# Vector-times-matrix products of a decode step: weights as the moving operand in column groups, one block transpose a layer, and two output banks

## The chip, the cores and the metric

The kernel runs on one core of a Trainium2 chip. The metric is the device time of one execution in microseconds (us), taken as the median of several runs. A separate execution is recorded by the hardware profiler; its span runs from the first to the last instruction. Engines are named as in the profile: PE (TensorE matmuls), PEld (TensorE weight loads), DVE (VectorE), ACT (ScalarE), POOL (GpSimd) and SP (SyncE, which here issues nearly all DMA transfers).

## The reference, cut to what matters

Two batch rows (B = 2, one new token each) go through an attention block with a long cache (A) and an MLP mixer (B); a gate mixes both. D = 1024, 32 heads of 128, 16384 cached positions, F = 3584, all in bf16.

```python
def _A_ref(x, k_cache, v_cache, wq, wo):
    q = (x @ wq).reshape(B, 1, 32, 128).transpose(0, 2, 1, 3)
    scores = jnp.einsum("bhqd,bhkd->bhqk", q, k_cache) * (128 ** -0.5)
    o = jnp.einsum("bhqk,bhkd->bhqd", softmax(scores), v_cache)
    return o.transpose(0, 2, 1, 3).reshape(B, 1, 4096) @ wo

def _B_ref(x, w1, w2, w3, w4):
    h = gelu(layernorm(x) @ w1)
    # g0..g3: the four quarters of h, each shifted by one or two steps along a sequence of length 1
    x1 = x + concatenate([g0, g1, g2, g3]) @ w2
    return x1 + gelu(layernorm(x1) @ w3) @ w4

g = sigmoid((A_x * gate_w).sum(-1))
out = g * A(A_x) + (1 - g) * B(A_x)
```

With a sequence of length 1 every shifted quarter is zero, and the kernel uses a zero tile for that input (`shT`).

## The kernel before, in words

The caches are 537 MB of the 573 MB that are moved. Work is cut into 32 **units** u = (pair of heads, batch row), each with 8.39 MB of K and 8.39 MB of V. SBUF holds one large tile `mem` of five **cells** of 32 KB a partition. A K or V block fills two cells: K of even units cells 0 and 1, of odd units cells 1 and 2; V cells 3 and 4 (V of unit 30 cells 0 and 1). The weights borrow the cells early on: `wq` cells 3 and 4, `w1` and `w2` cell 2, then `w3` cells 3 and 4, then `w4` the same two.

Every load stands in one queue, SP's, in the order of the program; a load waits on SP until the cells that it fills have been read, and those behind it wait too. The order is: wq (L125), x and gate weights (L127, L129), w1, w2 (L226), K0 (L97), w3 in two halves (L226), K1, the first rows of wo (L428), w4 in two halves (L226), K2, V0 in two halves (L104), K3, V1 (L100), K4 and so on. At the end stand V30, V31 in nine pieces (`load_v_pieces`, L112: seven of 1 MB and two of 0.5 MB) and the last four tiles of wo (`load_wo_last`, L436).

The main loop runs over n = 0 to 31. For unit n `score_chunks` transposes K on DVE in 32 x 32 blocks (L462, eight chunks a unit) and multiplies it on PE (L468); `softmax_a` to `softmax_c` transpose the scores on DVE (L489), exchange maxima over a product with a matrix of ones (L499), take the exponentials on ACT (L507) and sum (L521 or L529). `pv(n - 2)` multiplies the probabilities with V (L543): eight probability columns are stationary, V moves 512 columns at a time, and four such products go to four groups of 32 output partitions of the bank `oacc`. `pv_rows` (L559, L565) picks the wanted parts out of that bank on DVE; a product with `hsel` (L585, L590) turns them into columns, `OT`; and `wo_project` (L441) adds `OT` times two rows of wo to the output sum `arow`, in four groups of 256 columns that share one PSUM bank.

The small layers are what the change is about. **q** (L268) is computed with blocks of wq as the stationary operand and the two columns of x moving: 256 products into a tile of columns, then four products with a selection matrix `sel` (L281) and two copies (L292) that lay q out for the score weights. **LinearT** (w1 to w4, L233) works the same way, one 128 x 128 block stationary at a time; `compute(k, c0, c1)` does some output columns c of one half k of the rows, and its calls for w3 and w4 lie between the softmax steps of units 0 and 1. `mlp_post4` (L402) adds the MLP's result into `arow` over a product with an identity.

In the last unit, `pv_last` does V31's first three pieces as moving operand (L543), and the other six as stationary operand, 128 x 128 at a time (L612), each into the same two columns; `OT` of the last pair (L619) then releases `wo_project` for the pairs 14 and 15. Each of the four wo tiles is waited for by its own group of four products. The sum leaves PSUM in two halves, one on DVE (L677) and one on ACT (L678), and goes out over two queues (L680).

The tile framework arranges each engine's instructions at build time; on PE they don't always follow the order of the program (some products of `lin3` stand between score products of unit 0).

Of the kernel before, what the change touches and what calls it, by code (L numbers as in the profile page):

```python
# [10 lines left out]
FP32 = mybir.dt.float32  # L11
# [12 lines left out]
def kernel(  # L24
# [74 lines left out]
    def load_v(u):  # L99
        nc.sync.dma_start(out=region(v_cell[u], NJ * Dh), in_=cache_rows(A_v_cache, u))  # L100

    def load_v_half(u, k):
        at = slice(k * CELL, (k + 1) * CELL)
        nc.sync.dma_start(out=region(v_cell[u], NJ * Dh)[:, at], in_=cache_rows(A_v_cache, u)[:, at])  # L104

    PIECES = [32] * 7 + [16] * 2
    assert sum(PIECES) == NJ

# [29 lines left out]
    ones_f = const.tile([P, P], FP32)  # L138
    nc.vector.memset(ones_f[:], 1.0)

    sel = const.tile([P, 4, Q4, QP], BF16)
    nc.gpsimd.memset(sel[:], 0.0)
    for v in range(4):
        w, e = divmod(v, 2)
        nc.gpsimd.affine_select(
            out=sel[:, v],
            in_=sel[:, v],
            compare_op=ALU.not_equal,
            fill=1.0,
            base=-(2 * QP * w + e),  # L150
            pattern=[[0, Q4], [-2, QP]],
            channel_multiplier=1,
        )
    mask4 = const.tile([P, Q4], BF16)
    nc.gpsimd.memset(mask4[:], 1.0)
    nc.gpsimd.affine_select(
# [46 lines left out]
    for k in range(NP):  # L203
        t = const.tile([P, NJ // 4, 2, 4], BF16, name=f"pt{k}")
        nc.gpsimd.memset(t[:], 0.0)
        pts.append(t)

    class LinearT:

        def __init__(self, W, actT, name, cell, offset, nparts=1):  # L210
            self.actT = actT
            K, self.N = W.shape
            self.R = K // P
            self.C = self.N // P
            self.rows = self.R // nparts
            self.src = W.rearrange("(p r) n -> p (r n)", p=P)

            self.at = [(cell + k) * CELL + offset for k in range(nparts)]
            self.acc = mlp.tile([P, self.C, B], FP32, name=f"{name}_acc")

        def part(self, k):
            return mem[:, self.at[k] : self.at[k] + self.rows * self.N]

        def load(self, k=0):
            n = self.rows * self.N
            nc.sync.dma_start(out=self.part(k), in_=self.src[:, k * n : (k + 1) * n])  # L226

        def compute(self, k, c0, c1):
            wc = self.part(k).rearrange("p (r n) -> p r n", n=self.N)
            ps = misc_psum([P, c1 - c0, B])  # L230
            for c in range(c0, c1):
                for r in range(self.rows):
                    nc.tensor.matmul(  # L233
                        ps[:, c - c0, :],
                        lhsT=wc[:, r, :].rearrange("p (m c) -> p c m", c=self.C)[:, c, :],
                        rhs=self.actT[:, k * self.rows + r, :],
                        start=(r == 0),
                        stop=(r == self.rows - 1),
                    )
            acc = self.acc[:, c0:c1, :]  # L240
            if k == 0:
                nc.vector.tensor_copy(out=acc, in_=ps[:])
            else:
                nc.vector.tensor_tensor(out=acc, in0=acc, in1=ps[:], op=ALU.add)

    xn1T = mlp.tile([P, KC, B], BF16)
    hT = mlp.tile([P, KC, B], BF16)
# [5 lines left out]

    lin1 = LinearT(B_w1, xn1T, "w1", 2, 0)
    lin2 = LinearT(B_w2, shT, "w2", 2, KC * D)
    lin3 = LinearT(B_w3, xn2T, "w3", 3, 0, 2)
    lin4 = LinearT(B_w4, h2T, "w4", 3, 0, 2)
    lin1.load()
    lin2.load()
    load_k(0)  # L260
# [1 line left out]
    xT = const.tile([P, KC, B], BF16)  # L262
    nc.vector.tensor_copy(out=xT[:], in_=xin[:].rearrange("p b r -> p r b"))  # L263

    qps = misc_psum([P, H, B])
    for h in range(H):
        for r in range(KC):
            nc.tensor.matmul(  # L268
                qps[:, h, :],
                lhsT=wq_t[:, r, h * Dh : (h + 1) * Dh],  # L270
                rhs=xT[:, r, :],
                start=(r == 0),
                stop=(r == KC - 1),
            )
    lin3.load(0)
    lin3.load(1)
    qT = const.tile([P, H, B], BF16)
    nc.vector.tensor_copy(out=qT[:], in_=qps[:])
    qdps = misc_psum([P, 4, H * B])
    for v in range(4):  # L280
        nc.tensor.matmul(  # L281
            qdps[:, v, :],
            lhsT=sel[:, v].rearrange("p a k -> p (a k)"),
            rhs=qT[:].rearrange("p h b -> p (h b)"),
            start=True,
            stop=True,
        )

    qd = const.tile([P, HP, B, 4], BF16)
    for e in range(2):  # L290
        rows = slice(e * HALF, (e + 1) * HALF)
        nc.vector.tensor_copy(  # L292
            out=qd[rows],
            in_=qdps[rows].rearrange("p v (hp e b) -> p hp e b v", e=2, b=B)[:, :, e],
        )
    qdu = qd[:].rearrange("p hp b v -> p (hp b) v")

    def write_qw(u):
# [82 lines left out]
        layernorm_T(x1T[:], xn2T[:], "ln2")  # L381


    NQ = D // Q4
    arow_t = rps.tile([P, NQ], FP32, name="arow")
    nc.vector.memset(arow_t[:], 0.0)
    arow = [arow_t[QP * k : QP * k + B, :] for k in range(Q4)]

    def mlp_post4():

        omg = mlp.tile([P, B], FP32, name="omg")
        nc.vector.tensor_scalar(
            out=omg[:], in0=g_rep[:], scalar1=-1.0, scalar2=1.0, op0=ALU.mult, op1=ALU.add
        )
        nc.vector.tensor_tensor(out=bT[:], in0=lin4.acc[:], in1=x1T[:], op=ALU.add)
        nc.vector.tensor_tensor(
            out=bT[:], in0=bT[:], in1=omg[:].unsqueeze(1).to_broadcast([P, KC, B]), op=ALU.mult
        )
        W = NQ // KC
        for k in range(Q4):  # L400
            for c in range(KC):
                nc.tensor.matmul(  # L402
                    arow[k].rearrange("b (m c) -> b c m", c=KC)[:, c, :],
                    lhsT=bT[:, c, :],
                    rhs=ident_f[:, k * W : (k + 1) * W],
                    start=(c == 0),
                    stop=False,
                    skip_group_check=True,
                )
# [27 lines left out]

    def wo_project(hp):
        for r in range(2):
            for k in range(Q4):  # L440
                nc.tensor.matmul(  # L441
                    arow[k],
                    lhsT=OT[:, hp, r, :],
                    rhs=wo_tiles[hp, r][:, k * NQ : (k + 1) * NQ],
                    start=False,
                    stop=(hp == HP - 1 and r == 1),
                    skip_group_check=True,
                )
# [154 lines left out]
    def pv_last(u):  # L603
        hp, b = units[u]
        ot = misc_psum([P, 2])
        moving = sum(PIECES[:3]) // 4
        pv_moving(u, 0, moving, moving)
        red = pv_rows(u, mask4m)
        nc.tensor.matmul(ot[:], lhsT=red[:, 0:Dh], rhs=hsel[:], start=True, stop=False)
        V = v_view(u)  # L610
        for j in range(4 * moving, NJ):
            nc.tensor.matmul(  # L612
                ot[:],
                lhsT=V[:, j, :],
                rhs=pts[u % NP][:, j // 4, :, j % 4],
                start=False,
                stop=(j == NJ - 1),
            )
        nc.vector.tensor_tensor(out=OT[:, hp, :, b], in0=ot[:], in1=rinvs[u % NP][:], op=ALU.mult)  # L619
        for k in range(HP - LASTP, HP):  # L620
            wo_project(k)

    compute_gate()
    layernorm_T(xT[:], xn1T[:], "ln1")
    lin1.compute(0, 0, lin1.C)
    mlp_post1()
    lin2.compute(0, 0, lin2.C)
    mlp_post2()

    for n in range(NU):  # L630
# [6 lines left out]
        softmax_a(n)  # L637
        if n == 0:
            load_wo_pair(0)
            lin3.compute(0, 0, FC // 2)  # L640
            softmax_b(n)
            lin3.compute(0, FC // 2, FC)
            lin4.load(0)
            softmax_c(n)
            lin3.compute(1, 0, FC)
            lin4.load(1)
            gelu_T(lin3.acc[:], h2T[:], FC)
        elif n == 1:
            lin4.compute(0, 0, KC // 2)
            softmax_b(n)  # L650
            lin4.compute(0, KC // 2, KC)
            load_v_half(0, 0)
            softmax_c(n)
            lin4.compute(1, 0, KC)
            load_v_half(0, 1)
            mlp_post4()
        else:
            pv(n - 2)
            if n < NU - 1:
                load_v(n - 1)  # L660
            else:
                load_v_pieces(NU - 1)
            pv_end(n - 2)
            if n == NU - 1:
                load_wo_last()
            softmax_b(n)
            softmax_c(n)
# [3 lines left out]
    pv_end(NU - 2)  # L671
    pv_last(NU - 1)

    out_row = mlp.tile([P, NQ], BF16)
    used = slice(0, QP * (Q4 - 1) + B)
    half = NQ // 2
    nc.vector.tensor_copy(out=out_row[used, 0:half], in_=arow_t[used, 0:half])  # L677
    nc.scalar.activation(out=out_row[used, half:NQ], in_=arow_t[used, half:NQ], func=ACTF.Copy)  # L678
    for b, queue in ((0, nc.sync), (1, nc.scalar)):
        queue.dma_start(  # L680
            out=out[b, 0].rearrange("(k n) -> k n", k=Q4),
            in_=out_row[b : b + QP * (Q4 - 1) + 1 : QP, :],
        )


# [28 lines left out]
```

## Time and profile before

| | before |
|---|---|
| time, median of 3 runs | 1341.07 us (1340.96 to 1341.09) |
| the profiled execution's own time | 1341.09 us |
| its span | 1339.4 us |
| mean granted TensorE clock | 0.785 |
| busy: PE, PEld, DVE, ACT, POOL | 768.8, 351.9, 705.1, 105.2, 15.2 us |
| moved by DMA | 573.33 MB, mean 428 GB/s |
| queue q1 (SP's transfers) | 99.3% of 16 engines' span |

The profile gives busy time by engine, the span in 40 slices of 33.5 us each, the DMA queues, the chain of waits that ended last, and groups of instructions by line. The timeline lists instructions in order of time, neighbours merged: start, duration, engine, line, operation, output <- input, shape, count, and in brackets the idle time before with what ended it. `SPq` and `ACTq` are transfers issued by those engines; the duration there is that of issuing. A table by windows gives busy time, granted clock, DMA share and GB/s of each stretch.

### The profile page before, as it was taken

The page shows a single profiled execution, that of the slowest core. Times are in us where ns is not written, and L with a number is a line of the kernel's source. Part 1 is how long each engine was busy: PE and PEld are TensorE (multiplying, and loading weights), DVE is VectorE, ACT ScalarE, POOL GpSimd, SP SyncE. Part 2 cuts the span into 40 slices and gives each one's busy share as a digit, 9 for nine tenths or more (in the row PEclk, how much of TensorE's full clock was granted, in tenths as well). Part 3 has the DMA queues.
Part 4 walks back from the last instruction along what each step waited for, and adds up shares of the span by engine and source line. Part 5 has one row for each costly group of instructions (what it writes and reads, how often), then busy time and mean ns, then how long its engine had stood idle before and what let it go on. Part 6 is the DMA issues. An engine that isn't in the chain of part 4 may idle for free.

```text
span 1339.4 us, 12490 instructions
## 1 busy us (share of the span) xinstructions
PE 768.8 (57%) x5502; PEld 351.9 (26%) x5502; DVE 705.1 (53%) x695; ACT 105.2 (8%) x165; POOL 15.2 (1%) x54
## 2 busy tenths in 40 slices
PE   2688566554566645556654546665455665555564
PEld 2456222222222212222222212222122222222222
DVE  1445566554556554556655445656444665545561
ACT  0011000000000000000000000000000000000000
POOL 1000000000000000000000000000000000000000
PEclk9977887776788777788877778877678886777886
DMA  9999999999999999999999999999999999999997
GB/s 406 425 429 432 440 431 433 435 423 440 429 435 437 429 429 437 425 435 435 435 431 429 429 437 431 429 427 430 440 431 431 427 433 423 437 435 435 433 423 309
DMA packets 14486, 573.33 MB, mean 428 GB/s; under 512 B 1880, under 2 KB 1888, under 8 KB 4448
## 3 DMA queue, kind: packets, MB, share of 16 engines
q1 hardware_dynamic: 14424, 572.54, 99.3%
q8 instruction: 43, 0.70, 0.2%
q14 instruction: 11, 0.09, 0.0%
q10 hardware_dynamic: 8, 0.00, 0.0%
HBM read 572.53 MB, written 0.00 MB: 427 GB/s over the span
## 4 chain that ended last, share of the span: by engine, by line
DMA 67%; PE 16%; DVE 12%; issue 4%; ACT 0%; another core or an unknown queue 0%; POOL 0%; SPq 0%; ACTq 0%; DVEq 0%
DMA mem<-in_A_k_cache_dram 62%; PE S L468 12%; DVE KT L462 12%; PE misc L233 2%; DMA mem<-in_A_v_cache_dram 2%; DMA xin<-in_A_x_dram 2%; DMA wo<-in_A_wo_dram 1%; PE misc L268 1%; ACT pt L507 0%; PE arow L402 0%; PE oacc L543 0%; DVE St L489 0%; POOL ln_rstd L350 0%; PE misc L344 0%
## 5 line engine op out<-in xcount | busy, mean ns | idle before, releaser
L468 PE MATMUL S<-KT,qw 128*128 128x512 bf16 x2048 | 544.2, 415 | 369.5 <-DVE KT L462 369.3
L462 DVE STREAM_TRANSPOSE KT<-mem 128x2048 f32<-128x2048 f32 x256 | 570.9, 2283 | 271.7 <-DMA mem<-in_A_k_cache_dram 219.5
L468 PEld LDWEIGHTS <-qw 128*128 128x128 bf16 x2048 | 217.7, 107 | 688.3 <-issue 509.2
L543 PE MATMUL oacc<-mem,pt 128*8 128x512 bf16 x2008 | 116.9, 384 | 8.7 <-DMA mem<-in_A_v_cache_dram 8.7
L507 ACT ACTIVATE pt<-St,nb 64x256 bf16<-64x256 f32 x64 | 90.0, 1406 | 149.5 <-DVE nb L505 148.6
L493 ACT ACTIVATE Dm<-ident_s,m 128x128 f32<-128x128 f32 x32 | 12.8, 401 | 998.8 <-DVE m L491 998.8
L521 PE MATMUL misc<-rs,lmat 128*128 128x1 f32 x62 | 18.2, 362 | 85.8 <-ACT pt L507 85.6
L543 PEld LDWEIGHTS <-pt 128*8 128x8 bf16 x2008 | 46.4, 87 | 76.2 <-issue 25.9
L489 DVE STREAM_TRANSPOSE St<-S 128x512 f32<-128x512 f32 x32 | 22.9, 717 | 66.6 <-PE S L468 66.6
L523 DVE RECIPROCAL rinv<-misc 128x1 f32<-128x1 f32 x31 | 5.2, 169 | 96.3 <-PE misc L521 96.3
L559 DVE TENSOR_SCALAR part<-oacc,maskr 128x128 f32<-128x128 f32 x31 | 10.9, 351 | 83.0 <-PE oacc L543 83.0
L590 PE MATMUL misc<-hsel,red 128*128 128x2 f32 x112 | 17.5, 261 | 51.5 <-DVE red L565 51.5
L521 PEld LDWEIGHTS misc<-rs,lmat 128*128 128x128 f32 x62 | 15.5, 310 | 94.2 <-ACT pt L507 94.2
L233 PEld LDWEIGHTS <-mem 128*128 128x128 bf16 x576 | 36.9, 169 | 2.2 <-issue 1.4
L590 PEld LDWEIGHTS misc<-hsel,red 128*128 128x128 f32 x112 | 15.9, 202 | 64.8 <-issue 62.6
L507 ACT ACTIVATION_READ_ACCUMULATOR pt<-St,nb 64x1 f32 x64 | 30.7, 480 | 0.0
L565 DVE SCALAR_TENSOR_TENSOR part<-oacc,maskr,part 128x128 f32<-128x128 f32 x62 | 21.8, 351 | 2.2
L268 PE MATMUL misc<-xT,mem 128*128 128x2 bf16 x256 | 7.1, 165 | 26.1 <-DVE xT L263 23.5
L301 POOL TENSOR_TENSOR qw<-qd,mask 128x16 bf16<-128x16 bf16 x32 | 8.4, 264 | 1188.1 <-PE S L468 1159.5
L599 DVE CAST OT<-misc 64x2 bf16<-64x2 f32 x56 | 9.0, 160 | 22.9 <-PE misc L590 22.6
L499 PE MATMUL misc<-Dm,ones_f 128*128 128x128 f32 x64 | 16.5, 343 | 3.5 <-ACT Dm L493 3.5
L505 DVE TENSOR_REDUCE nb<-misc 64x1 f32<-64x64 f32 x64 | 14.2, 222 | 5.5 <-PE misc L499 3.5
(97 smaller groups left out, 150.7 us busy)
## 6 DMA issues: line engine op xcount, KB each, us to landing
mem<-in_B_w_dram SPq DMA_DIRECT2D x4, 3584.0 KB, 18.8
mem<-in_A_v_cache_dram SPq DMA_DIRECT2D x2, 4096.0 KB
wo<-in_A_wo_dram SPq DMA_DIRECT2D x7, 1024.0 KB, 32.4
mem<-in_A_v_cache_dram SPq DMA_DIRECT2D x7, 1024.0 KB, 24.7
mem<-in_B_w_dram SPq DMA_DIRECT2D x2, 2048.0 KB, 28.6
mem<-in_A_v_cache_dram SPq DMA_DIRECT2D x2, 512.0 KB, 17.9
wo<-in_A_wo_dram SPq DMA_DIRECT2D x4, 256.0 KB, 12.8
mem<-in_A_k_cache_dram SPq DMA_DIRECT2D x32, 28.2
```

The lines of the kernel that those rows point to most:

```text
L233: nc.tensor.matmul(ps[:, c - c0, :], lhsT=wc[:, r, :].rearrange("p (m c) -> p c m", c=self.C)[:, c, :], rhs=self.actT[:, k * self.rows + r ...
L268: nc.tensor.matmul(qps[:, h, :], lhsT=wq_t[:, r, h * Dh : (h + 1) * Dh], rhs=xT[:, r, :], start=(r == 0), stop=(r == KC - 1),)
L462: nc.vector.transpose(out=kt[:], in_=Kc.rearrange("p j d -> p (j d)").bitcast(FP32))
L468: nc.tensor.matmul(S, lhsT=t[:, v, NG - 1 - m : NG - 1 - m + P], rhs=ktb[:, half * GT : (half + 1) * GT, w, :, e], start=(first and n == 0 ...
L489: nc.vector.transpose(out=st[:].rearrange("p j r -> p (j r)"), in_=S[:])
L499: nc.tensor.matmul(R_ps[:], lhsT=ones_f[:], rhs=Dm[:], start=True, stop=True)
L505: nc.vector.tensor_reduce(out=nb[rows], in_=R_ps[rows, rows], axis=AX.X, op=ALU.min)
L507: nc.scalar.activation(out=Pt[rows, :, e, :].rearrange("p (m a) k -> p a k m", a=GT // 4), in_=st[rows, :, 0:NG].rearrange("p (a k) m -> p ...
L521: nc.tensor.matmul(tot_ps[:, 0:1], lhsT=lmat[:], rhs=rs[:], start=True, stop=True)
L543: nc.tensor.matmul(acc[QP * q : QP * q + 8, :], lhsT=pts[u % NP][:, g].rearrange("p h k -> p (h k)"), rhs=v_view(u)[:, 4 * g : 4 * g + 4, ...
L565: nc.vector.scalar_tensor_tensor(out=red[:] if twice else part[:], in0=in0.unsqueeze(1).to_broadcast([P, 2, Dh]) if twice else in0, scalar ...
L590: nc.tensor.matmul(ot[:, r, :], lhsT=red[:, r : 2 * Dh : 2], rhs=hsel[:], start=True, stop=True,)
```

## The change

Four things are edited together.

1. **q and w1 to w4 with the weights moving.** The two columns of the activation become the stationary operand; the weights move, up to 512 columns at a time, and four products go to four groups of 32 output partitions of one `oacc` bank (two banks take turns, `flip`). For q the column groups hold heads of even and odd place, each twice. For a linear layer each group holds a quarter of the columns. The bank is read out whole: for q straight by a DVE block transpose (`flipped`), for a linear layer by a copy on ACT or DVE into `wide` and then one block transpose for the layer. `sel`, its POOL instructions and its four products go away.
2. **One load and one computation a layer.** w3, w4 and V0 are each loaded by one DMA in place of two halves; `lin3.compute()` and `lin4.compute()` are one call each, and w4's load stands behind all of lin3, V0's behind all of lin4.
3. **The last V.** Seven of V31's nine pieces move (56 groups, was 24); the last two are stationary. The product that turns the moved part into columns is put behind these and behind `wo_project` of pair 14.
4. **The output sum in two groups.** `arow` becomes two tiles of 512 columns, on partitions 0 and 1 of one PSUM tile and 32 and 33 of another; `wo_project` does two products of 512 columns a tile in place of four of 256, and `mlp_post4` half as many products. The memset of `arow` goes away. At the end DVE copies the one half and SP stores it, ACT copies the other and stores it.

```diff
+    def flip():
+        flips[0] += 1
+        return oacc[flips[0] % 2]
+
+    def flipped(src, n):
+        t = mlp.tile([P, FC * QP], FP32, tag="flip", name="flip")[:, 0:n]
+        nc.vector.transpose(out=t, in_=src)
+        return t.rearrange("p (c k) -> p c k", k=QP)[:, :, 0:B]
...
-        def compute(self, k, c0, c1):
...
+        def compute(self):
+            n = QP * self.C
+            step = QP
+            while step * self.C > 512:
+                step //= 2
+            w = step * self.C
...
+            for m in range(n // w):
+                at = slice(m * w, (m + 1) * w)
+                acc = flip()
+                for r in range(self.R):
+                    for g in range(Q4):
+                        nc.tensor.matmul(
+                            acc[QP * g : QP * g + B, 0:w],
+                            lhsT=self.actT[:, r, :],
+                            rhs=wc[:, r, g, at],
+                            start=(r == 0),
+                            stop=(r == self.R - 1),
+                        )
+                if m % 2 == 0:
+                    nc.scalar.activation(out=wide[:, at], in_=acc[:, 0:w], func=ACTF.Copy)
+                else:
+                    nc.vector.tensor_copy(out=wide[:, at], in_=acc[:, 0:w])
+            got = flipped(wide.rearrange("p (k c) -> p c k", c=self.C), n)
+            nc.vector.tensor_copy(out=self.acc[:], in_=got)
...
+    for h0 in range(0, HP, HG):
+        acc = flip()
         for r in range(KC):
...
+            for g in range(Q4):
+                nc.tensor.matmul(
+                    acc[QP * g : QP * g + B, :],
+                    lhsT=xT[:, r, :],
+                    rhs=wq_t[:, r, :].rearrange("p (hp e d) -> p hp e d", e=2, d=Dh)[
+                        :, h0 : h0 + HG, g // 2, :
+                    ],
...
+        got = flipped(acc[:].rearrange("p (c k e) -> p c e k", k=QP, e=2), 512)
         nc.vector.tensor_copy(
...
+            out=qd[:, h0 : h0 + HG],
+            in_=got.rearrange("p (hp v) b -> p hp b v", v=4),
+        )
+    lin3.load()
...
-        moving = sum(PIECES[:3]) // 4
+        moving = sum(PIECES[:-2]) // 4
...
-        nc.tensor.matmul(ot[:], lhsT=red[:, 0:Dh], rhs=hsel[:], start=True, stop=False)
...
+        for k in range(HP - LASTP, HP - 1):
+            wo_project(k)
+        nc.tensor.matmul(ot[:], lhsT=red[:, 0:Dh], rhs=hsel[:], start=False, stop=True)
         nc.vector.tensor_tensor(out=OT[:, hp, :, b], in0=ot[:], in1=rinvs[u % NP][:], op=ALU.mult)
-        for k in range(HP - LASTP, HP):
-            wo_project(k)
+        wo_project(HP - 1)
...
             load_wo_pair(0)
-            lin3.compute(0, 0, FC // 2)
+            lin3.compute()
+            lin4.load()
             softmax_b(n)
-            lin3.compute(0, FC // 2, FC)
-            lin4.load(0)
+            gelu_T(lin3.acc[:], h2T[:], FC)
             softmax_c(n)
...
-            lin4.compute(0, 0, KC // 2)
+            lin4.compute()
+            load_v(0)
             softmax_b(n)
...
+    nc.vector.tensor_copy(out=out_row[0:B, :], in_=arow[0])
+    nc.sync.dma_start(out=rows[:, 0:512], in_=out_row[0:B, :])
+    nc.scalar.activation(out=out_row[QP : QP + B, :], in_=arow[1], func=ACTF.Copy)
+    nc.scalar.dma_start(out=rows[:, 512:1024], in_=out_row[QP : QP + B, :])
```

More of the change, by code (lines that the diff above doesn't have):

```diff
@@ L100, in load_v @@
         nc.sync.dma_start(out=region(v_cell[u], NJ * Dh), in_=cache_rows(A_v_cache, u))
-    def load_v_half(u, k):
-        at = slice(k * CELL, (k + 1) * CELL)
-        nc.sync.dma_start(out=region(v_cell[u], NJ * Dh)[:, at], in_=cache_rows(A_v_cache, u)[:, at])
     PIECES = [32] * 7 + [16] * 2
@@ L139 @@
     nc.vector.memset(ones_f[:], 1.0)
[L141 to L153, printed above, removed]
     mask4 = const.tile([P, Q4], BF16)
@@ L206, with __init__ @@
         pts.append(t)
+    flips = [0]
+    def flip():
[5 more added lines that the diff above has]
+        return t.rearrange("p (c k) -> p c k", k=QP)[:, :, 0:B]
     class LinearT:
-        def __init__(self, W, actT, name, cell, offset, nparts=1):
+        def __init__(self, W, actT, name, cell, offset):
             self.actT = actT
@@ L214, in __init__ @@
             self.C = self.N // P
-            self.rows = self.R // nparts
             self.src = W.rearrange("(p r) n -> p (r n)", p=P)
-            self.at = [(cell + k) * CELL + offset for k in range(nparts)]
+            at = cell * CELL + offset
+            self.dst = mem[:, at : at + self.R * self.N]
             self.acc = mlp.tile([P, self.C, B], FP32, name=f"{name}_acc")
[L221 to L226, printed above, removed]
@@ L228, in compute, with load @@
-        def compute(self, k, c0, c1):
[L229 to L244, printed above, removed]
+        def load(self):
+            nc.sync.dma_start(out=self.dst, in_=self.src)
@@ new lines, in compute @@
+        def compute(self):
[4 more added lines that the diff above has]
+            w = step * self.C
+            wide = mlp.tile([P, FC * QP], FP32, tag="wide", name="wide")[:, 0:n]
+            wc = self.dst.rearrange("p (r g n) -> p r g n", g=Q4, n=n)
+            for m in range(n // w):
[16 more added lines that the diff above has]
+            nc.vector.tensor_copy(out=self.acc[:], in_=got)
@@ L255 @@
     lin2 = LinearT(B_w2, shT, "w2", 2, KC * D)
-    lin3 = LinearT(B_w3, xn2T, "w3", 3, 0, 2)
-    lin4 = LinearT(B_w4, h2T, "w4", 3, 0, 2)
+    lin3 = LinearT(B_w3, xn2T, "w3", 3, 0)
+    lin4 = LinearT(B_w4, h2T, "w4", 3, 0)
     lin1.load()
@@ L263 @@
     nc.vector.tensor_copy(out=xT[:], in_=xin[:].rearrange("p b r -> p r b"))
-    qps = misc_psum([P, H, B])
-    for h in range(H):
+    qd = const.tile([P, HP, B, 4], BF16)
+    HG = 512 // Dh
+    for h0 in range(0, HP, HG):
+        acc = flip()
         for r in range(KC):
[L268 to L286, printed above, removed]
-        )
[L289 to L295, printed above, removed]
+            for g in range(Q4):
[5 more added lines that the diff above has]
+                    ],
+                    start=(r == 0),
+                    stop=(r == KC - 1),
+                )
+        got = flipped(acc[:].rearrange("p (c k e) -> p c e k", k=QP, e=2), 512)
+        nc.vector.tensor_copy(
+            out=qd[:, h0 : h0 + HG],
+            in_=got.rearrange("p (hp v) b -> p hp b v", v=4),
+        )
+    lin3.load()
     qdu = qd[:].rearrange("p hp b v -> p (hp b) v")
@@ L381, in mlp_post2 @@
         layernorm_T(x1T[:], xn2T[:], "ln2")
[L384 to L387, printed above, removed]
+    NH2 = D // 512
+    arow_t = [rps.tile([QP * k + B, 512], FP32, name=f"arow{k}") for k in range(NH2)]
+    arow = [arow_t[k][QP * k : QP * k + B, :] for k in range(NH2)]
     def mlp_post4():
@@ L398, in mlp_post4 @@
         )
-        W = NQ // KC
-        for k in range(Q4):
+        W = 512 // KC
+        for k in range(NH2):
             for c in range(KC):
@@ L439, in wo_project @@
         for r in range(2):
-            for k in range(Q4):
+            for k in range(NH2):
                 nc.tensor.matmul(
@@ L443, in wo_project @@
                     lhsT=OT[:, hp, r, :],
-                    rhs=wo_tiles[hp, r][:, k * NQ : (k + 1) * NQ],
+                    rhs=wo_tiles[hp, r][:, k * 512 : (k + 1) * 512],
                     start=False,
@@ L615, in pv_last @@
                 rhs=pts[u % NP][:, j // 4, :, j % 4],
-                start=False,
-                stop=(j == NJ - 1),
-            )
+                start=(j == 4 * moving),
+                stop=False,
+            )
+        for k in range(HP - LASTP, HP - 1):
+            wo_project(k)
+        nc.tensor.matmul(ot[:], lhsT=red[:, 0:Dh], rhs=hsel[:], start=False, stop=True)
         nc.vector.tensor_tensor(out=OT[:, hp, :, b], in0=ot[:], in1=rinvs[u % NP][:], op=ALU.mult)
-        for k in range(HP - LASTP, HP):
-            wo_project(k)
+        wo_project(HP - 1)
     compute_gate()
     layernorm_T(xT[:], xn1T[:], "ln1")
-    lin1.compute(0, 0, lin1.C)
+    lin1.compute()
     mlp_post1()
-    lin2.compute(0, 0, lin2.C)
+    lin2.compute()
     mlp_post2()
@@ L639 @@
             load_wo_pair(0)
-            lin3.compute(0, 0, FC // 2)
+            lin3.compute()
+            lin4.load()
             softmax_b(n)
-            lin3.compute(0, FC // 2, FC)
-            lin4.load(0)
+            gelu_T(lin3.acc[:], h2T[:], FC)
             softmax_c(n)
-            lin3.compute(1, 0, FC)
-            lin4.load(1)
-            gelu_T(lin3.acc[:], h2T[:], FC)
         elif n == 1:
-            lin4.compute(0, 0, KC // 2)
+            lin4.compute()
+            load_v(0)
             softmax_b(n)
-            lin4.compute(0, KC // 2, KC)
-            load_v_half(0, 0)
+            mlp_post4()
             softmax_c(n)
-            lin4.compute(1, 0, KC)
-            load_v_half(0, 1)
-            mlp_post4()
         else:
@@ L672 @@
     pv_last(NU - 1)
[L674 to L683, printed above, removed]
+    out_row = mlp.tile([QP + B, 512], BF16)
+    rows = out.rearrange("b s d -> (b s) d")
+    nc.vector.tensor_copy(out=out_row[0:B, :], in_=arow[0])
+    nc.sync.dma_start(out=rows[:, 0:512], in_=out_row[0:B, :])
+    nc.scalar.activation(out=out_row[QP : QP + B, :], in_=arow[1], func=ACTF.Copy)
+    nc.scalar.dma_start(out=rows[:, 512:1024], in_=out_row[QP : QP + B, :])
 _INS = ['A_x', 'A_k_cache', 'A_v_cache', 'A_wq', 'A_wo', 'B_x', 'B_w1', 'B_w2', 'B_w3', 'B_w4', 'gate_w']
```

## The prediction

> **What bounds the kernel.** I read the page's 40 slices first, then the DMA queues, then the issues of SP's queue over the first 250 us, and last the timeline of the final 30 us.
>
> ```profile
> span 1339.4 us, 12490 instructions
> ...
> PE 768.8 (57%) x5502; PEld 351.9 (26%) x5502; DVE 705.1 (53%) x695; ACT 105.2 (8%) x165; POOL 15.2 (1%) x54
> ...
> GB/s 406 425 429 432 440 431 433 435 423 440 429 435 437 429 429 437 425 435 435 435 431 429 429 437 431 429 427 430 440 431 431 427 433 423 437 435 435 433 423 309
> ...
> q8 instruction: 43, 0.70, 0.2%
> ```
>
> Only the first slice (406 GB/s) and the last (309) leave the plateau around 431; no compute engine is over 57% busy. So the span is bytes over rate, and an edit counts only in three ways: it lets SP's queue run dry, it changes what the DMA engines must carry, or it lengthens what follows the last byte. The change's bytes are the same.
>
> **Does the queue run dry?** That is a matter of how early each load is issued.
>
> ```profile
> 64.42 0.33 SPq L97 DMA_DIRECT2D mem<-in_A_k_cache_dram  x1
> 64.79 0.43 SPq L428 DMA_DIRECT2D wo<-in_A_wo_dram  x1
> 83.35 7.85 SPq L226 DMA_DIRECT2D mem<-in_B_w_dram  x2
> 102.99 0.33 SPq L97 DMA_DIRECT2D mem<-in_A_k_cache_dram  x1
> 121.31 7.77 SPq L104 DMA_DIRECT2D mem<-in_A_v_cache_dram  x2
> ```
>
> ```profile
> 53.45 4.50 DVE L462 STREAM_TRANSPOSE KT<-mem 128x2048 f32<-128x2048 f32 x2 [3.55 <-DMA mem<-in_A_k_cache_dram]
> ...
> 129.26 4.50 DVE L462 STREAM_TRANSPOSE KT<-mem 128x2048 f32<-128x2048 f32 x2
> ```
>
> K0 is there at 53.4. At 431 GB/s w3 (2 x 3584 KB, 7.34 MB) takes 17.0 us, a K or V block (8.39 MB) 19.5, a wo pair (1.05 MB) 2.4. So the backlog ends: w3 at 70.4, K1 89.9, wo 92.3, w4 109.3, K2 128.8. K2's first use at 129.26 confirms the count. By the windows a transfer moves its first bytes about 1 us after its issue (wq issued at 0.79; nothing moved in the first us, 721 GB/s in the second). Before, the slack of each issue against the end of the backlog is therefore K1 6.0 us, w4 8.9, K2 6.3, V0 7.5, each less 1.
>
> **The change, part by part.**
>
> *q.* Out go 256 products (7.1 us in two stretches, with 2.61 us between them in which PE waited for nothing the profile shows), four products with `sel` (0.39) and three copies (0.22 + 0.59). In come 128 products of 512 columns, four at a time. The nearest rows are the probability products of L543: 64 in 3.63 us at granted clock 1.0, and, in the pair of weight-load rows shown for the end below, four per 0.43 us at 0.50. That is 7.3 to 13.7 us; four block transposes like L489's (0.72 each) and four copies of some 0.25 follow, all but the last beside the products. q would be done between 32 and 39 instead of 34.5, w3 issued between 31 and 38 instead of 33.1. Its backlog reaches to 53.4: cost nothing, cover 14 us.
>
> The Trainium skill, "TensorEngine Tiling (Array Packing)", section "PSUM Bottleneck", speaks against this edit: after a fourfold TensorE gain the PSUM copy may become the bottleneck. By that rule the four evacuations, not the products, would set q's length. No row of the trace before shows which, and by either q ends under the cover just named.
>
> *w1, w2.* 64 + 64 products (3.98 us each) become 32 + 32 of 256 columns (0.9 to 1.7 us each), an ACT copy of 256 (0.3 to 0.45, from 0.28 for 128 columns at L678 and 0.40 at L493), a transpose of some 0.4 and a copy of 0.17. The chain ended at 49.9, before K0; it stays there within 3 us and nothing but lin3 waits for its result.
>
> *w3, then w4's load.* 224 products (2.07 + 1.69 + 3.66 + 7.22 = 14.6 us) become 64 of 448 columns: 3.2 us at clock 1.0, 6.0 at 0.50. Two copies out of PSUM (some 0.6 each), a transpose of 896 columns (0.72 x 896/512 = 1.25) and a copy follow. w4 waits for all of it. At the earliest lin3 runs when w3 is there, 70.4; at the latest behind the maxima's product (ended at 79.8), so w4 is issued by 85.8 against 92.3: slack 5.5 after the 1 us. Queued behind it on SP are K2 and V0. K2 profits: DVE started unit 1 only at 92.49 because it stood behind the gelu chain of lin3; now it can start when K1 is there, 89.9.
>
> *w4, then V0's load.* 224 products (14.0 us) become 112 of 256: 3.2 to 6.0 us. In the worst place, behind the maxima's product of unit 1 (ended at 117.97), V0 is issued at 124.6 with the sum's product before it, against 128.8: slack 3.2 us. This is the thinnest cover in the change; without it each us is paid in full. Behind V0 on SP stands K3, whose slack was 9.5 (issued at 138.97, V0's bytes end at 148.3).
>
> All DVE work that is added is some 8 us, in the first 125 us, where DVE waits for K or for PE. The later `wo_project`s halve in number, hidden like the rest of the middle.
>
> *Instruction fetch.* q8's 0.70 MB over 43 packets fit PE's 11,004 instructions at 64 B, 256 a packet. Its 0.2% of 16 engines' span is 43 us, 1.0 us a packet. Out go 128 + 4 (q), 32 + 32 + 160 + 112 (layers), 32 (L402), 64 (wo), 96 (last V): 660 products with their weight loads, 1320 instructions, 5.2 packets. Spread over 16 engines that is 0.33 us. In the last 8 us the engines finish unevenly (267, 225, 159, then 20 GB/s in 2-us windows from 1328 on), so the gain at the end depends on who is late: 0 if a late engine serves no fetches, 1.0 if it loses a whole packet. I take 0.35.
>
> *The end.*
>
> ```profile
> 1303.68 0.59 PE L529 MATMUL misc<-rs,ones_f 128*128 128x2 f32 x2 [3.45 <-DVE rs L526]
> ...
> 1313.30 0.14 PEld L543 LDWEIGHTS <-pt 128*8 128x8 bf16 x4 [0.28 <-issue]
> 1313.73 0.14 PEld L543 LDWEIGHTS <-pt 128*8 128x8 bf16 x4 [0.28 <-issue]
> ...
> 1332.80 0.59 PE L612 MATMUL misc<-pt,mem 128*128 128x2 bf16 x16 [0.68 <-DMA mem<-in_A_v_cache_dram]
> ...
> 1333.42 0.16 DVE L619 TENSOR_TENSOR OT<-misc,rinv 128x2 bf16<-128x2 f32 x1 [10.34 <-PE misc L612]
> 1333.46 0.38 PE L441 MATMUL arow<-wo,OT 128*2 128x256 bf16 x4
> 1334.11 0.38 PE L441 MATMUL arow<-wo,OT 128*2 128x256 bf16 x4 [0.27 <-DMA wo<-in_A_wo_dram]
> ...
> 1335.42 0.38 PE L441 MATMUL arow<-wo,OT 128*2 128x256 bf16 x4 [0.26 <-DMA wo<-in_A_wo_dram]
> ...
> 1335.86 0.29 DVE L677 CAST out_row<-arow 98x128 bf16<-98x128 f32 x1 [2.27 <-PE arow L441]
> 1336.18 0.28 ACT L678 ACTIVATE out_row<-arow 98x128 bf16<-98x128 f32 x1 [32.82 <-DVE out_row L677]
> ...
> 1336.49 1.35 ACTq L680 DMA_DIRECT2D out_dram<-out_row  x1
> ```
>
> ```profile
> 1332.00:1334.00 2.00, 1.09 (x25) 0.71 (x23) 0.16 (x1) 0.00 (x0) 0.00 (x0) 0.50 0.43 159
> ```
>
> Before, PE keeps up: each wo tile releases four products and the last, landed at 1335.42, is followed by 0.41 us of PE. The reader should see that the last piece of V (1332.80) is not what ends the kernel, so the shorter V work gains nothing by itself: 128 stationary products that finish between arrivals become 32 moving ones at 0.43 for four (0.85 a piece, pieces 2.45 us apart). The moved part is complete at 1330.30 + 0.85 + 0.2; four DVE operations (1.64 us, as at 1321.45) make `red` by 1333.0, in time.
>
> New order: the stationary tail ends at 1333.39; pair 14 does its first tile until 1333.9 and its second, landed at 1334.11, until 1334.54; then `red`'s product, priced by L529 at 0.59 (by L609 at 0.38 when PE was at 1.0): 1335.13; `OT` 0.22: 1335.35; pair 15 then has two tiles of 512 columns, 0.43 each, plus some 0.17 to drain (0.38 less the 0.21 that 256 columns take): 1336.4. That is 0.55 after today's 1335.83. If `red`'s weights load beside the products and its price is the lower, the last tile's own landing binds, 1335.42 + 0.60 = 1336.02, so +0.2 at the least.
>
> The read-out: DVE's copy of 512 columns is 0.69 (0.291 for 128 and 1.05 ns a column more, from L278's 0.224 for 64), ACT's 0.59 (0.8 ns a column, from L365's two shapes). Side by side, the ACT store, the last to be issued, starts 0.65 after PE's end, as today's 0.66. One behind the other, as L678 waited for L677, it is 1.37: +0.7. I take side by side, since each copy reads its own tile.
>
> The Trainium skill, "PSUM — Partial Sum Buffer", section "PSUM bank collisions raise a hardware error ⚠️", has two engines' accesses to one bank and partition quadrant kept apart by a dependency, ACT against DVE too. The trace agrees for one shared tile: ACT starts 0.03 us after DVE ends. By the rule two banks carry no such wait and the sum stays as above; were the wait there all the same, it would be 0.7 more.
>
> **Sum.** Middle 0, fetches -0.35, end +0.55: +0.2 on the span, 1339.6; with the 1.7 us outside the span (1341.09 of the profiled execution less 1339.4; the median of the runs is 1341.07) it is **1341.3 us**. The bounds are -1.0 + 0.2 and 0 + 0.55 + 0.7: 1340.3 to 1342.35.
>
> **The rivals.** *The queue runs dry (slower).* V0 is held until lin4 is done. The loss begins when that is after 127.8 us and reaches 2.7 us at 130.5. If products with two stationary columns did not run four at a time, lin3 would take 64 x 0.37 = 23.9 us at clock 0.50 and end at 103.7 against 91.3, 12.4 late; lin4's 23.9 would start when w4 is there, 121.7, and V0 be 5.4 late: 1341.1 + 17.8 = 1359. For it: the wait for the whole layer is new, and PE's order is rearranged at build time, so a layer could be put in a bad place. Against: L441's four products with two columns take 0.38 together, and slack was 5 us and more everywhere. Chance 6%, of it 5% over 2.7 us.
>
> *The end is dearer.* Copies in turn and no fetch gain: +1.25, 1342.4; for it the one wait seen, against it the two tiles. 14%.
>
> *The fetches were what made the late engines late.* If these lose one packet or two and the end costs 0.2: 1340.3 or 1339.3. For it: the uneven finish; against: 5.2 packets are few. 15%, faster all the same by less than 0.2%. Something unseen that gains more: 3%.
>
> *The change doesn't do what it says at the end.* PE ran 31 products of lin3 at 66.20, amid unit 0's scores, so `red`'s product may be put before pair 14's: then the last landing binds, +0.2 - 0.35, 1340.9. This lies inside my forecast's own range, 1340.5 to 1342.0, which has 62%.
>
> **Chances.** About 0.2%, 2.7 us, is what a measurement of this kernel can tell from no change. Faster by more 3%, within 91%, slower by more 6%. The range 1339.9 to 1342.8 takes in most of the two small cases.
>
> **What would show it.** Right: 43 fetch packets become 38; every slice but the ends stays near 431 GB/s; w4 and V0 are issued before 91 and 127; PE's last product ends 0.2 to 0.6 after the last wo tile's arrival allows, and the two copies overlap. Wrong: a slice among the first five well under 425, a copy that waits for the other, or a last wo tile that lands over 1 us from 1335.4.

## The result, and the profile after

| | before | after |
|---|---|---|
| time, median of 22 runs each | 1341.12 us | 1339.21 us (1339.08 to 1339.52) |
| ratio after / before | | 0.9986 (95% interval 0.9979 to 0.9992) |
| span of the profiled execution | 1339.4 us | 1337.4 us |
| PE instructions, products + weight loads | 11,004 | 9,684 |
| packets of PE's fetch queue q8 | 43 | 38 |
| first product of the last wo tile | 1335.42 us | 1333.69 us |

The change gains 1.9 us, 0.14%. That is within the 0.2% that I gave 91%, but outside the range (1339.9 to 1342.8), and its sign is the other one than that of the 0.2 us forecast. The page after:

```profile
span 1337.4 us, 11166 instructions
...
PE 753.6 (56%) x4842; PEld 314.7 (24%) x4842; DVE 711.9 (53%) x700; ACT 106.9 (8%) x169; POOL 13.9 (1%) x49
...
GB/s 408 436 423 440 428 434 432 436 426 437 434 430 440 423 434 432 438 438 420 438 424 438 436 434 434 420 435 430 441 428 432 436 422 430 436 436 432 426 431 321
...
q8 instruction: 38, 0.62, 0.2%
q14 instruction: 11, 0.09, 0.0%
```

The plateau is where it was, and only the first and the last slice sag, as before; five fetch packets are gone, as counted. A fetch packet brings an engine its next instructions, and the queues q8 and q14 carry them: q8's 0.62 MB are 9,684 PE instructions of 64 B. The loads of the early part, in SP's timeline after (w4, K2 and V0):

```profile
77.68 0.33 SPq L217 DMA_DIRECT2D mem<-in_B_w_dram  x1
100.81 0.33 SPq L97 DMA_DIRECT2D mem<-in_A_k_cache_dram  x1
122.75 0.33 SPq L100 DMA_DIRECT2D mem<-in_A_v_cache_dram  x1
```

Against the backlog's ends of 92.3, 109.3 and 128.8 the slack, less 1 us, is 13.6, 7.5 and 5.1 us. The chain of waits after, in its last stretch (start, duration, what):

```profile
1323.58 10.07 DMA wo<-in_A_wo_dram
1333.65 0.04 issue
1333.69 0.63 PE arow L433 x2
1334.32 0.67 DVE out_row L663
```

And the timeline of the end after:

```profile
1331.52 0.57 PE L612 MATMUL misc<-hsel,red 128*128 128x2 f32 x2
1332.01 0.09 PEld L433 LDWEIGHTS <-OT 128*2 128x2 bf16 x3
1332.01 2.27 PE L433 MATMUL arow<-wo,OT 128*2 128x512 bf16 x8
...
1334.31 0.68 DVE L663 CAST out_row<-arow 2x512 bf16<-2x512 f32 x1 [2.03 <-PE arow L433]
1334.34 0.59 ACT L665 ACTIVATE out_row<-arow 2x512 bf16<-2x512 f32 x1 [31.50 <-PE arow L433]
1334.96 0.53 ACTq L666 DMA_DIRECT2D out_dram<-out_row  x1
1335.02 0.33 SPq L664 DMA_DIRECT2D out_dram<-out_row  x1
```

Three readings. The product of `red` (L612) stands ahead of pair 14's products, not behind them as in the program; so the last tile's landing binds. The two copies start within 0.03 us of each other. And the store that ACT issues takes 0.53 us to issue, not 1.35. The difference of the spans adds up along this chain: last tile -1.73 (1335.42 to 1333.69), PE behind it +0.22 (0.41 to 0.63), PE's end to ACT's store 0 (0.66 to 0.64), from ACT's store to the end of the span -0.5 (2.9 to 2.4): -2.0.

What remains to be explained is the first term, five times what I gave it. The bytes of the loads are the same, and neither kernel let the queue run dry.

### The profile page after: what moved, and what is told of

Same layout as the page of the kernel before. It is cut to its first block, busy times and chain, and to the rows that moved or that the text cites. A ratio compares the mean times of both kernels' runs of the same rounds, so it can differ in the third digit from the quotient of the medians.

```text
span 1337.4 us, 11166 instructions
## 1 busy us (share of the span) xinstructions
PE 753.6 (56%) x4842; PEld 314.7 (24%) x4842; DVE 711.9 (53%) x700; ACT 106.9 (8%) x169; POOL 13.9 (1%) x49
## 4 chain that ended last, share of the span: by engine, by line
DMA 73%; PE 12%; DVE 12%; issue 4%; SPq 0%
DMA mem<-in_A_k_cache_dram 70%; DVE KT L454 11%; PE S L460 11%; DMA mem<-in_A_v_cache_dram 2%; DMA wo<-in_A_wo_dram 1%; PE oacc L535 0%; SPq L217 0%; DVE out_row L663 0%; PE arow L433 0%; SPq L125 0%; SPq L123 0%; SPq L121 0%
## 5 line engine op out<-in xcount | busy, mean ns | idle before, releaser
L535 PE MATMUL oacc<-mem,pt 128*8 128x512 bf16 x2040 | 120.1, 387 | 13.3 <-DMA mem<-in_A_v_cache_dram 13.3
L274 PE MATMUL oacc<-mem,xT 128*2 128x512 bf16 x128 | 8.3, 426 | 23.4 <-DVE xT L265 23.4
L557 DVE SCALAR_TENSOR_TENSOR red<-oacc,maskr,part 128x256 f32<-128x256 f32 x31 | 15.0, 484 | 1.1
```

What stands on the lines that cost most here:

```text
L535: nc.tensor.matmul(acc[QP * q : QP * q + 8, :], lhsT=pts[u % NP][:, g].rearrange("p h k -> p (h k)"), rhs=v_view(u)[:, 4 * g : 4 * g + 4, ...
L557: nc.vector.scalar_tensor_tensor(out=red[:] if twice else part[:], in0=in0.unsqueeze(1).to_broadcast([P, 2, Dh]) if twice else in0, scalar ...
```

## Experiments

The trace has a clue. DVE's first transpose of each unit starts when K has landed whole, so it marks whichever DMA engine is last. From one unit to the next that is 38.7 us, 2.5 more where a wo pair lies between. Some units are a further step late. The timeline of the kernel after, units 12 to 14:

```profile
522.30 2.31 DVE L454 STREAM_TRANSPOSE KT<-mem 128x2048 f32<-128x2048 f32 x1 [6.58 <-DMA mem<-in_A_k_cache_dram]
...
561.02 2.31 DVE L454 STREAM_TRANSPOSE KT<-mem 128x2048 f32<-128x2048 f32 x1 [7.03 <-DMA mem<-in_A_k_cache_dram]
...
600.96 2.31 DVE L454 STREAM_TRANSPOSE KT<-mem 128x2048 f32<-128x2048 f32 x1 [7.60 <-DMA mem<-in_A_k_cache_dram]
```

38.72, then 39.94: a step of 1.2 us. In the records of the DMA packets such a late interval holds, in the traces before and after alike, q8's packet 9, 17, 25 or 33. After, these begin at 292.3, 584.4, 864.4 and 1168.5 us, and late are the K of units 7, 14, 21 and 29 (326.1, 601.0, 878.5, 1194.7); before, they begin at 150.1, 429.9, 717.2 and 1014.1, and late are units 3, 10, 17 and 25. Packet 41 of the kernel before begins at 1296.4, behind the K of the last unit; the kernel after has none. This made **theory F**: the last load ends when one DMA engine ends, that engine serves one PE fetch packet in eight, and each costs it over a microsecond. The profile names no DMA engine, so the engine is inferred; what the runs can test is the packet's number. The rivals were that the merged loads and the shorter end made the gain (**M**), and that each packet costs all engines a little (the averaged price of the prediction).

**More fetches, nothing else.** The kernel after with small products that nobody reads, a number k of them behind each softmax of units 2 to 31:

```diff
+    padw = const.tile([P, P], BF16)
+    nc.gpsimd.memset(padw[:], 0.0)
+    def pad(k):
+        ps = misc_psum([P, 2])
+        for _ in range(k):
+            nc.tensor.matmul(ps[:], lhsT=padw[:], rhs=padw[:, 0:2], start=True, stop=True)
...
             softmax_c(n)
+            pad(34)
```

> The changed kernel with 34 extra small products (128x128 stationary, 2 columns moving, result never read) behind the softmax of each unit from 2 to 31: 1020 products with their weight loads, 2040 instructions, 8 more fetch packets (38 to 46) and nothing else. Theory F (the last load's end is set by one DMA engine that serves the fetches in turn with seven others, 1.2 us a packet, as unit 14's K comes 1.2 us late against its neighbours): one packet more on that engine, last wo tile 1.0 to 1.3 us later than 1333.7, time 1340.3 to 1340.6 against 1339.2 of the changed kernel. Theory M (the gain came from the merged loads and the shorter end): no change, 1339.2. The predicted mean price over 16 engines: +0.5, 1339.7.

> The same with 68 products a unit, 4080 instructions, 16 more packets (54). Theory F: two packets more on the late engine, +2.0 to +2.5, time 1341.2 to 1341.7, and 1.0 to 1.3 above the run with 46 packets. Theory M: 1339.2. Mean over 16 engines: +1.0, 1340.2.

Measured: 1340.77 us with 46 packets and 1342.26 with 54, so +1.56 and +3.05. M's "no change" did not come, and the averaged price falls too (+0.5 and +1.0 were its numbers). The step is 1.5 us, above the 1.0 to 1.3 expected of F. In these traces the late units follow the same packet numbers, five of them in the first kernel (the last is 41) and six in the second (49). The pads stand in every unit from 2 on, so a cost of their own work on PE would have shown in every unit. What the merged loads and the end are worth is for the next runs. Differences of 0.1 us between runs mean nothing: the kernel before took 1341.08 to 1341.21 beside them.

**The loads undone.** w3, w4 and V0 each in two transfers again, issued together:

```diff
-        def load(self):
-            nc.sync.dma_start(out=self.dst, in_=self.src)
+        def load(self, parts=1):
+            n = self.R * self.N // parts
+            for k in range(parts):
+                at = slice(k * n, (k + 1) * n)
+                nc.sync.dma_start(out=self.dst[:, at], in_=self.src[:, at])
...
```

> The changed kernel with w3, w4 and V0 each loaded by two transfers, issued one behind the other at the same place. Theory F: at most the 0.5 us that stood between the two kernels before the first missing packet, so 1339.2 to 1339.7. Theory M: the whole shift of the last landing comes back, last wo tile 1.0 to 1.7 us later, 1340.2 to 1340.9.

Measured: 1339.23 us, the last tile's products at 1333.98 instead of 1333.69. Merging the loads is worth nothing that the median shows; the 0.3 us of landing are those of one execution, itself 0.2 slower than the profiled one of the kernel after.

**The output sum undone.** The four groups in one bank, with their memset, copies and stores, as in the kernel before (the lines of the kernel before put back; here the first of them):

```diff
-    NH2 = D // 512
-    arow_t = [rps.tile([QP * k + B, 512], FP32, name=f"arow{k}") for k in range(NH2)]
+    NQ = D // Q4
+    arow_t = rps.tile([P, NQ], FP32, name="arow")
+    nc.vector.memset(arow_t[:], 0.0)
...
```

> The changed kernel with the output sum as before: four groups of 256 columns in one bank, memset, copies of 98 rows, stores of four rows a queue. 80 products more (64 of wo, 16 of the MLP's), 160 instructions, 0.6 packets. Theory F for the landing: unchanged or one packet (0 or +1.2). For the end itself: PE 0.2 us shorter behind the last tile, copies 0.05 us shorter in turn, the ACT store's issue 1.35 instead of 0.53 us: net +0.4 to +0.6 if the store's issue counts in full, -0.2 if it does not. Time 1339.6 to 1339.8 with the landing unchanged and the issue counting, 1339.0 without.

Measured: 1339.53 us, with 39 packets. The timeline of its end:

```profile
1334.04 0.38 PE L434 MATMUL arow<-wo,OT 128*2 128x256 bf16 x4 [0.26 <-DMA wo<-in_A_wo_dram]
1334.47 0.29 DVE L665 CAST out_row<-arow 98x128 bf16<-98x128 f32 x1 [1.84 <-PE arow L434]
1334.80 0.28 ACT L666 ACTIVATE out_row<-arow 98x128 bf16<-98x128 f32 x1 [31.36 <-DVE out_row L665]
1335.10 0.65 SPq L668 DMA_DIRECT2D out_dram<-out_row  x1
1335.11 1.36 ACTq L668 DMA_DIRECT2D out_dram<-out_row  x1
```

ACT waits for DVE again and its store takes 1.36 us to issue again; the span ends at 1338.0, 2.9 us behind that issue, against 2.4 in the kernel after. The two-group sum gains 0.3 us net by the medians, and it fits that the issue counts, less PE's shorter products. This run does not prove the split: the landing is 0.35 later in its profile.

**Steps or a slope.** The pads of 270 and 660 products give 40 and 43 packets, on either side of the 41st.

> The changed kernel with 9 extra small products a unit (270, 540 instructions): 40 fetch packets instead of 38. In the six traces so far the K that comes late always follows packet 9, 17, 25, 33 or 41, so the engine that ends last takes one in eight. Theory S (steps): 40 packets still miss the 41st, no change: 1339.2 (within 0.2). Theory A (each packet costs the same, 0.19 us as the runs with 46 and 54 packets have it on average): 1339.6.

> The changed kernel with 22 extra products a unit (660, 1320 instructions): 43 packets, as many as the kernel before has, with the change's loads, layers and end kept. Theory S: the 41st packet is there, the whole step of the run with 46: 1340.6 to 1340.8. Theory A: 5 x 0.19, 1340.15.

Measured: 1339.33 and 1340.69 us. Three packets cost 1.36 us, two before them 0.12. The timelines of the last units' K (29, 30, 31), first with 40 packets, then with 43:

```profile
1195.65 4.51 DVE L454 STREAM_TRANSPOSE KT<-mem 128x2048 f32<-128x2048 f32 x2 [6.66 <-DMA mem<-in_A_k_cache_dram]
...
1234.36 4.50 DVE L454 STREAM_TRANSPOSE KT<-mem 128x2048 f32<-128x2048 f32 x2 [6.84 <-DMA mem<-in_A_k_cache_dram]
...
1273.03 4.50 DVE L454 STREAM_TRANSPOSE KT<-mem 128x2048 f32<-128x2048 f32 x2 [6.38 <-DMA mem<-in_A_k_cache_dram]
```

```profile
1195.41 4.50 DVE L454 STREAM_TRANSPOSE KT<-mem 128x2048 f32<-128x2048 f32 x2 [6.91 <-DMA mem<-in_A_k_cache_dram]
...
1234.10 4.50 DVE L454 STREAM_TRANSPOSE KT<-mem 128x2048 f32<-128x2048 f32 x2 [6.12 <-DMA mem<-in_A_k_cache_dram]
...
1274.36 4.50 DVE L454 STREAM_TRANSPOSE KT<-mem 128x2048 f32<-128x2048 f32 x2 [8.54 <-DMA mem<-in_A_k_cache_dram]
```

With 43 packets unit 31 comes 40.26 us after unit 30, with 40 it comes 38.67 after. The step is the 41st packet, and the last tile's products follow it, in the two chains of waits:

```profile
1334.26 0.63 PE arow L433 x2
...
1335.59 0.63 PE arow L433 x2
```

The kernel before had that packet, the kernel after has not. The kernel with 43 packets also has as many as the kernel before and all the rest of the change. It takes 1340.69 us against 1341.21 beside it, so 0.52 us of the gain have nothing to do with the packets, and the other 1.4 are the packets'.

**Halves of the change.** Parts 1 and 2 alone (the kernel after with `pv_last` and the output sum of the kernel before), and parts 3 and 4 alone (the kernel before with those two of the kernel after):

> Only the first two parts of the change (q and the layers with moving weights, one load a layer); V31 with six stationary pieces and the output sum as before. 10068 PE instructions, 40 packets. Theory S: the last landing is that of the changed kernel within 0.4, the end that of the kernel before: 1339.4 to 1339.8. Theory A: 3 packets less, 1340.5.

> Only the last two parts (V31 moving to the last two pieces, output sum in two groups) on the kernel before. 10620 PE instructions, 42 packets. Theory S: the 41st is there, landing unchanged; the end alone changes, 0.2 us more on PE and 0.5 less in the stores: 1340.7 to 1340.9. Theory A: a further 0.2 less, 1340.5 to 1340.7.

Measured: 1339.55 us with 39 packets, the last tile's products at 1333.83; and 1340.71 us with 41 (one packet fewer than counted in both), the last tile's products at 1335.41, as before the change (1335.42). The first half moves the landing and the second only the end: 1.66 and 0.50 us less than the kernel before on the same chip (1341.21), a little over the whole change's 1.91 when added. The 0.50 of the second half agrees with the 0.52 that the run with 43 packets left to the rest.

**Can the landing be had earlier still?** Two questions on the uneven ends of the engines. First, both wo tiles of pair 15 in row blocks that don't divide evenly among 16:

```diff
-                nc.sync.dma_start(out=t[:, k, r, :], in_=wo_heads[:, H - 4 + 2 * k + r, :])
+                src = wo_heads[:, H - 4 + 2 * k + r, :]
+                for rows in [slice(0, 119), slice(119, P)] if k == 1 else [slice(0, P)]:
+                    nc.sync.dma_start(out=t[rows, k, r, :], in_=src[rows])
```

> The changed kernel with each of the two wo tiles of pair 15 loaded in two transfers, rows 0 to 118 and rows 119 to 127, so that the first can only be shared out evenly to 7 (or 17, or 1) engines. In the trace seven engines are through with their packets 4 to 5 us ahead of the last one. If the rows go to engines that are early, the late ones carry 2 x 16 KB less, 1.2 us at 64 KB in 2.42 us: last landing about 1332.5, time 1338.0 to 1338.6. If they go to engines that are late, these carry 2 x 18.5 KB more, 1.4 us: 1340.4 to 1341.0. If the landing does not depend on the engines' unequal ends, 1339.2 to 1339.5.

Measured: 1342.1 us, the last tile's products at 1336.34: 2.65 us later, more than the second case gave. The run doesn't say why. The profile doesn't name the engines that these rows went to; and the split changed the issue as well. SP had six transfers to issue instead of four, over 13.24 us instead of 7.79, and in the chain of waits the last transfer begins at 1329.60 instead of 1323.58:

```profile
1329.60 6.70 DMA wo<-in_A_wo_dram
```

Second, whether the fetches of the other engines' instructions (q14, 8 KB each) fall on a late engine. A first kernel put 18 DVE memsets of two columns into each unit:

> The changed kernel with 18 extra DVE memsets of two columns a unit (540 instructions), so 4 more packets in the fetch queue q14 (11 to 15), 8 KB each, and none in q8. If the engine that ends last serves q14 too, each costs what 8 KB take, 0.3 us or more: up to +1.2, 1340.4; if it serves q8 alone, no change: 1339.2 to 1339.4.

Measured: 1352.03 us (1349.85 to 1353.45 in four runs), and this says nothing on q14, because the memsets wait for nothing and were arranged at build time, 531 of the 540 into the first 104 us of DVE. Two rows of DVE's timeline:

```profile
90.25 13.55 DVE L658 MEMSET dpad<- 128x2 f32 x107
103.84 2.31 DVE L454 STREAM_TRANSPOSE KT<-mem 128x2048 f32<-128x2048 f32 x1
```

Two windows (busy PE, PEld, DVE, ACT, POOL, then clock, DMA share, GB/s):

```profile
105.00:110.00 5.00, 3.81 (x10) 1.28 (x10) 3.96 (x11) 0.00 (x0) 0.00 (x0) 0.50 0.85 367
110.00:115.00 5.00, 4.26 (x19) 1.78 (x18) 5.00 (x3) 0.00 (x0) 0.00 (x0) 0.99 0.04 15
```

K of unit 1 waited behind 107 memsets, K2 was issued at 114.34 instead of 100.81, and for some 5 us next to nothing moved. V0 followed at 135.72 instead of 122.75, and from 134 to 136 the loads stood at 8 GB/s again. At unit 3 K is 10.6 us late (177.87 against 167.30), nearly all that this execution lost (1349.85 against 1339.11). This is the slower rival's mechanism, at K2's place as well as V0's: what an early load is late beyond the backlog's end was not won back.

The second kernel repeats the reciprocal that each unit needs anyway, which binds the added work to its place:

```diff
-            nc.vector.reciprocal(out=rinv[:, 0:1], in_=tot_ps[:, 0:1])
+            for _ in range(19 if u > 1 else 1):
+                nc.vector.reciprocal(out=rinv[:, 0:1], in_=tot_ps[:, 0:1])
```

> The changed kernel with the reciprocal of units 2 to 30 done 19 times in place of once (29 x 18 = 522 DVE instructions, 0.17 us each, bound to their place by the sum that they read): 4 more packets in the fetch queue q14, none in q8, and no load issued late. If the engine that ends last serves q14 too: up to 0.3 us a packet, 1339.5 to 1340.4. If it serves q8 alone: 1339.2 to 1339.4. The 3.1 us more of DVE work a unit is hidden behind the loads in either case.

Measured: 1341.96 us, K2 and V0 issued at 100.72 and 122.63 as in the kernel after. Its fetch queues and the last of its chain:

```profile
q8 instruction: 38, 0.62, 0.2%
q14 instruction: 15, 0.12, 0.0%
```

```profile
1326.43 10.03 DMA wo<-in_A_wo_dram
1336.46 0.04 issue
1336.50 0.63 PE arow L433 x2
```

Four more packets of 8 KB made the last tile 2.8 us late, 0.7 us a packet and over twice the most that I expected. The late units now follow packets of q14 (from unit 10 on, eight steps of 0.76 to 0.97 us, behind packets that begin some 105 to 120 us apart; none at q8's 17 and 33). So an engine that serves DVE's fetches ends late too, and in the kernel after it cannot be far from the last: four steps of 0.95 would be 3.8 us, of which 2.8 show at the end, so it ends there about 1.0 us before the last, by this estimate. That shortening PE's instruction stream further would soon gain nothing without DVE's follows from this, but was not tried.

No kernel that was run beats the kernel after.

## Why the prediction was right or wrong

**Right: the middle costs nothing.** The slack rows above show it, with the columns moving four at a time: q's 128 products took 8.34 us, lin3's 64 3.20, lin4's 112 5.19. V0 was issued 1.9 us earlier than my worst place. The build did put lin4 into that place, behind the maxima's and the sum's products (117.50). The run with the memsets shows what the cover is worth when it is gone.

**Wrong, a size: the fetches.** The mechanism was named and the packets were counted right (43 to 38). The step that failed is "Spread over 16 engines that is 0.33 us ... I take 0.35", with its bounds of 0 and 1.0. The measured term is -1.4 to -1.5 (1339.33 and 1339.21 against the 1340.69 of 43 packets). An average over engines is the wrong price where the last one decides: the packets that count are one in eight, so the price is a step, 1.36 us between 40 and 43 packets, 1.5 for each eight more than 38 (1.56 and 3.05), and the change crossed one step. Of the -1.73 that the landing moved in the two traces, 1.24 lie behind the last unit's K, where packet 41 stands; the other 0.49 are there already at that K (1272.93 and 1272.44), the medians leave no room for them, and their cause is open. The upper bound was too low as well: I took a packet at 1.0 us, and the packets' own records do take 1.0 to 1.1, but a late unit comes mostly 1.2 to 1.5 late. What I had named as a sign of being wrong, a last tile over 1 us from 1335.4, is what came.

My third rival, late engines that lose one or two packets, had the right cause and 15%; it gave 1340.3 for one packet because a packet was priced at 1.0 and the end at +0.2, with nothing gained in the stores. That its 1339.3 for two packets lies near the measured time is luck: one step was crossed, not two.

**Wrong, a size: the end.** The sum has +0.55 here, and the runs show -0.25 in the traces (+0.22 on PE, -0.47 behind the store) and -0.3 to -0.5 in the medians (1339.53 against 1339.21 with the old sum, 1340.71 against 1341.21 with parts 3 and 4 alone). "That is 0.55 after today's 1335.83" rested on the program's order. The build put `red`'s product ahead of pair 14's, which was my fourth case, and its +0.2 is what PE shows (0.41 to 0.63). The copies are as priced, 0.68 and 0.59, and run side by side. The Trainium skill, "PSUM — Partial Sum Buffer", section "PSUM bank collisions raise a hardware error ⚠️", has the wait between ACT and DVE for a shared bank and quadrant alone; the trace agrees, 0.03 us between the two starts with two banks, 0.32 with one.

**Missed: the stores.** I set the start of ACT's store at 0.65 after PE's end, which is right (0.64), and gave its issue no term. It shrank from 1.35 to 0.53 us with half as many rows a store, and the span ends 0.5 earlier behind it; that the issue is what shortens the end was not tested by itself. The parts 3 and 4 alone gain their 0.4 to 0.5 us here, PE's +0.2 included.

**Right: q's read-outs stay hidden.**

```profile
23.41 8.34 PE L274 MATMUL oacc<-mem,xT 128*2 128x512 bf16 x128 [23.41 <-DVE xT L265]
...
28.35 0.72 DVE L201 STREAM_TRANSPOSE flip<-oacc 128x512 f32<-128x512 f32 x1 [0.78 <-PE oacc L274]
29.10 0.20 DVE L284 CAST qd<-flip 128x32 bf16<-128x32 f32 x1
30.08 0.72 DVE L201 STREAM_TRANSPOSE flip<-oacc 128x512 f32<-128x512 f32 x1 [0.78 <-PE oacc L274]
```

Each of q's four groups is read by a transpose of 0.72 us and a copy of 0.20, and the transposes start 1.73 us apart; those shown wait 0.78 us for PE. The Trainium skill, "TensorEngine Tiling (Array Packing)", section "PSUM Bottleneck", warns that the PSUM copy may become the bottleneck; here the products set the pace.

## What to carry to other kernels

In a kernel that is bound by transfers from end to end, the last landing decides, and what delays the last of the DMA engines counts in full: here PE's and DVE's instruction fetches, in steps. Count the instructions that an edit adds or removes on every engine, divide by the packet (256 of PE's here), and look for a step, instead of pricing by the mean over all engines.

To test a suspected fixed cost, add it in doses and look for steps; and bind added work to the data of its place, since work that waits for nothing is moved to the front.

## What the runs showed of the hardware that I had not expected

- The late units follow PE fetch packets 9, 17, 25, 33, 41 and 49 in the traces with 38 to 54 of them, those with more DVE instructions apart. It looks as if the fetches went round eight DMA engines in turn; the profile doesn't say which engine takes which.
- The unit behind such a packet of 16 KB came mostly 1.2 to 1.5 us late, twice and more what 16 KB take at the plateau's rate for one engine (431/16 = 27 GB/s, 0.6 us); behind one of 8 KB from q14 it was 0.76 to 0.97 us, where the bytes take 0.3.
- A store of two rows a queue took ACT 0.53 us to issue and SP 0.33; one of four rows 1.35 and 0.65.
- Left open: some 0.5 us by which the kernel before is late at units 8, 9, 23 and 24, where both kernels have had as many steps. The run with split loads is 0.2 to 0.3 late there. Part may be the single execution's: four kernels that differ by their pads alone reach unit 7 between 326.22 and 326.60.
